# Block-sparse attention with a fused feed-forward on one core: sums of squares a step later, raw-query loads behind the query copies, and scores beside AV at the end of a step

## The chip, the cores and the metric

The kernel runs on one core of one Trainium2 chip. The core has five engines that run their own instruction streams and wait for each other by semaphores: TensorE (PE in the profile, with its weight loads shown apart as PEld), VectorE (DVE), ScalarE (ACT), GpSimd (POOL) and SyncE (SP), which here only issues DMAs. Transfers run on 16 DMA engines. The metric is device microseconds of one execution. A profile is one execution taken by the hardware profiler; its span runs from its first to its last instruction.

## The reference, cut to what matters

Four batches of eight heads, 768 tokens, head size 64. Queries and keys are cut into blocks of 32. A query block sees its own and its two neighbour blocks, the first and the last block, and three sampled blocks; the first and last query blocks see all. The attention output of all heads is the input of a two-layer feed-forward net.

```python
scores = scale * np.matmul(q, k.transpose(0, 1, 3, 2))
scores = np.where(mask, scores, -1000000000.0)
scores = scores - np.max(scores, axis=-1, keepdims=True)
attn = np.exp(scores)
attn = attn / (np.sum(attn, axis=-1, keepdims=True) + 1e-09)
attn_out = np.matmul(attn, v)
...
x = np.ascontiguousarray(attn_out.transpose(0, 2, 1, 3)).reshape(B * S, H * D)
h = x @ w_in                      # 3072 x 512 @ 512 x 2048
g = np.maximum(0.01 * h, h)
return (g @ w_out).astype(np.float32)
```

## The kernel before

**Numbers.** Every float32 operand is scaled by a power of two and split into two float16 halves, so that TensorE runs in float16: high times high, plus the two cross products. The scale comes from a sum of squares: ScalarE squares a raw tile with an accumulated row sum (L544 for keys, L575 for queries, L480 for values), TensorE sums the rows over the partitions by a matmul with ones (L131; tiles q_sum, k_sum, v_sum), VectorE makes the scale (L145 to L154), and then ScalarE writes the high half and VectorE the low half (L556 and L558 for keys, L582 and L584 for queries).

**Queries.** A half item of 128 query rows is loaded raw into rq (one buffer, so a load waits until the half item before has been split), split into qa, turned by a DMA transpose into qs (L587), and copied twice, with its upper and lower partitions exchanged, into qxs (L589, L590). The scores need qs and qxs. Keys go the same way into kt (transpose L562), values go through DRAM (scr) and come back gathered as vg. kg is the gathered keys of one query tile; GpSimd copies the sampled blocks into it (L644).

**Units, pairs and steps.** A unit is two heads of one 64-query tile; two units are a pair. The loop over all 192 units makes one step per unit. Twelve items (4 batches of 3) have 16 units each, so step 32 begins item 0_2 (batch 0, third item), and names read batch_item_tile_headpair. A unit runs through scores s (L702), the row minimum and scaled copy p (L711, DVE), the exponential (L723, ACT), the norm r (L734, L735), the high half pp (L750, ACT), the low half pp (L771, DVE), one DMA transpose per pair into pt (L776), and AV (L803) into the bank av. In the first item TensorE turns instead (tile turn). A tile of av is then evacuated into x.

**Feed-forward.** An item that has its four tiles makes eight chunks. A chunk is 24 matmuls h (L838), ht on ACT (L844), leaky maximum and cast g on DVE (L847, L851), the low half of g on GpSimd (L852), and 12 matmuls o (L865). The first two items run it weight quarter by weight quarter while the weights are still being decoded from float64 on ACT and DVE (tiles W and wbuf, L344 to L423); from about 230 us on the weights are there.

**What sets the order.** Each step walks through the letters of a string in CFG and emits what each letter stands for: t is L711 of this unit; d, i, s are norm, high half and low half of earlier units; x the exponential; S the scores of the next pair, in a pair's second step; c, m, g the activation of a chunk; o its second matmuls; v the evacuation; a AV of a pair whose low half was made three steps ago; p the side work on queries, keys and values; w the weights; h a chunk's first matmuls. What is emitted gets a priority by its place, and a scheduler that simulates the engines while the program is built then fixes each engine's order; so a moved letter can move other work too. Side work runs in generators that give back a cost at each yield; a step has a quota of 1.2 (1.6 in the first 16 steps), and a generator that has used it up goes on in the next step. SyncE's queue holds all direct loads, transposes and copies in one order, and a DMA whose data is not ready holds those behind it.

**What sizes the waits.** The scores have two buffers in PSUM, so a pair's scores wait until L711 has read the pair before; pt has three buffers, p four, rq one, kg and vg two, x three.

Of the kernel before, what the change touches and what calls it, by code (L numbers as in the profile page):

```python
# [43 lines left out]
    "lead0": 2,  # L44
    "ob": 4,
    "ord": "dtsixScmgovabphw",
    "p": 4,
    "pe_t": 1,
    "pp": 3,
# [19 lines left out]
def tile_block_sparse_attention_ffn(  # L69
# [19 lines left out]
    nc = tc.nc  # L89
# [129 lines left out]
    last_sp = {}  # L219
# [4 lines left out]
    def behind(begin, name):  # L224
        for i in nc.cur_bb.bb.instructions[begin:]:
            if name:
                tc.add_manual_dep(i, name, mybir.DependencyInfo(
                    mybir.DependencyClass.NoSync, mybir.DependencyReason.DATA), reason="order")
# [281 lines left out]
    def load_q(b, j, i):  # L510

        t = pa.tile([P, H, D], F32, tag="rq", name=f"rq_{b}_{j}_{i}", bufs=CFG["rq"])
        lo = j * N2 - BLOCK + i * P
        src = lambda a, n: q[b, :, a:a + n, :].rearrange("h t d -> t h d")
        if lo < 0:
            nc.sync.dma_start(out=t[:BLOCK], in_=src(0, BLOCK))
            nc.sync.dma_start(out=t[BLOCK:Q2], in_=src(S - BLOCK, BLOCK))
            nc.sync.dma_start(out=t[Q2:], in_=src(BLOCK, Q2))
        else:
            nc.sync.dma_start(out=t, in_=src(lo, P))  # L520
        return t
# [13 lines left out]
    def prep_k(b, hp, rk):  # L535

        nm = f"k{b}_{hp}"
        ss = sm.tile([P, 1], F32, tag="ssk", name=f"ss_{nm}")
        if b == 0:
            k16 = early_k.bitcast(F16)[:, (NP + hp) * 2 * S:(NP + hp + 1) * 2 * S].rearrange(  # L540
                "p (n l d) -> p n l d", n=HC, l=2)
        else:
            k16 = pa.tile([P, HC, 2, D], F16, tag="k16", name=f"k16_{nm}", bufs=1)
        nc.scalar.activation(flat(k16)[:, :S], flat(rk), AF.Square, accum_out=ss)  # L544
        yield 1.0
        yield 0.01
        pb = scale_sum(ss, 1, nm)
        yield 0.2
        inv, s = scale_of(pb, 1, nm, fl="k")
        if (b, "inv") not in kready:  # L550
            kready[b, "inv"] = cst.tile([P, NP], F32, name=f"kinv_{b}")
        nc.vector.tensor_scalar(
            out=kready[b, "inv"][:, hp:hp + 1], in0=inv[:, :1], scalar1=-SCALE, scalar2=None, op0=ALU.mult)
        yield 0.4
        raw = rk.rearrange("p h c d -> p (h c) d")
        nc.scalar.activation(k16[:, :, 1, :], raw, AF.Copy, scale=s[:, :1])  # L556
        yield 1.0
        nc.vector.scalar_tensor_tensor(  # L558
            out=k16[:, :, 0, :], in0=raw, scalar=s[:, :1], in1=k16[:, :, 1, :], op0=ALU.mult, op1=ALU.subtract)
        if b not in kts:  # L560
            kts[b] = pa.tile([P, H, S], F16, tag="kt", name=f"kt_{b}", bufs=2)
        nc.sync.dma_start_transpose(  # L562
            out=kts[b][:, 2 * hp:2 * hp + 2, :].rearrange("p h (c t) -> p (h c) t", t=P),
            in_=k16.rearrange("p n l d -> p (n l d)"))
        if b == 0:
            last_sp["k", hp] = latest()
        kready[b, hp] = True
        yield 1.2

    def prep_q(b, j, i, rq):  # L570

        nm = f"q{b}_{j}_{i}"
        ss = sm.tile([P, 1], F32, tag="ssq", name=f"ss_{nm}")
        qa = pa.tile([P, H, 2, D], F16, tag="qa", name=f"qa_{nm}", bufs=1)
        nc.scalar.activation(flat(qa)[:, :H * D], rq.rearrange("p h d -> p (h d)"), AF.Square, accum_out=ss)  # L575
        yield 0.7
        yield 0.01
        pb = scale_sum(ss, 1, nm)
        yield 0.2
        inv, s = scale_of(pb, 1, nm)  # L580
        yield 0.4
        nc.scalar.activation(qa[:, :, 1, :], rq, AF.Copy, scale=s[:, :1])  # L582
        yield 0.7
        nc.vector.scalar_tensor_tensor(  # L584
            out=qa[:, :, 0, :], in0=rq, scalar=s[:, :1], in1=qa[:, :, 1, :], op0=ALU.mult, op1=ALU.subtract)
        qs = pa.tile([P, H, P], F16, tag="qs", name=f"qs_{nm}", bufs=2)
        nc.sync.dma_start_transpose(out=qs, in_=flat(qa))  # L587
        qxs = pa.tile([P, H, P], F16, tag="qxs", name=f"qxs_{nm}", bufs=2)
        nc.sync.dma_start(out=qxs[:D], in_=qs[D:])  # L589
        nc.sync.dma_start(out=qxs[D:], in_=qs[:D])  # L590
        last_sp["q"] = latest()
        qstack[b, j, i] = (qs, qxs, inv)
        yield 0.8
# [329 lines left out]
    def until(key, ready):  # L923
        while not ready():
            assert next(gens[key], "end") != "end" or ready(), key
# [84 lines left out]
    def get_q(n):  # L1010
        if n < len(halves):
            if n >= CFG["rq"]:
                until(("q", *halves[n - CFG["rq"]]), lambda: halves[n - CFG["rq"]] in qstack)
            rq[n] = load_q(*halves[n])

    def start_q(n):
        if n < len(halves):
# [59 lines left out]
    step = 0  # L1077
# [44 lines left out]
    for u in units:  # L1122
# [33 lines left out]
        if step == 0:  # L1156
            scores([u])
        c = aq[0] if aq else None
        for w in CFG["ord"]:
            if w == "c" and c:  # L1160
                ffn_act1(c)
            elif w == "m" and c:
# [130 lines left out]
```

## Time and profile before

| | |
|---|---|
| three runs | 866.07 us median (863.73 to 870.84) |
| the profiled execution | 863.27 us, span 861.6 us |
| mean granted TensorE clock | 0.948 |
| VectorE busy | 598.1 us in 1595 instructions |
| ScalarE busy | 512.4 us in 1199 instructions |
| GpSimd busy | 353.5 us in 472 instructions |
| DMA | 135.33 MB, mean 157 GB/s, q1 (SyncE's queue) 64.9% of 16 engines' span |

The span falls into three parts. Up to about 230 us the weights are loaded and decoded, attention of batch 0 runs beside it, and TensorE's granted clock swings between full and half. From 230 us to about 800 us one attention step and half a feed-forward chunk alternate on TensorE. The last 60 us are the last items' feed-forward alone. In a view of waits, a row gives the waiting engine and line, what it waited for, the total, the number and the longest. In a timeline, a row gives start, duration, engine, line, operation, tiles and count, and in brackets the idle time before it. A view of windows gives each engine's busy time per stretch, then the granted clock and the share of DMA.

### The profile page before, as it was taken

The numbers are of one execution on the slowest core, as the hardware profiler recorded it, in microseconds if no ns is written. First come the engines' busy times: TensorE is split into PE (matmuls) and PEld (weight loads), VectorE is DVE, ScalarE is ACT, GpSimd is POOL, SyncE is SP. The second block draws the span as 40 slices with busy tenths as digits, with TensorE's granted clock in tenths as the row PEclk, the third lists the DMA queues.
The fourth block names the chain that finished last, engine by engine and source line by source line (L and its number), as shares of the span: only waits on it lengthen the run. The fifth ranks groups of instructions, "written<-read, shape, count | busy, mean of one in ns | idle before, by whom it ended". The sixth has DMA issues, their size and how long they took to land.

```text
span 861.6 us, 20081 instructions
## 1 busy us (share of the span) xinstructions
PE 753.5 (87%) x7140; PEld 499.7 (58%) x7140; DVE 598.1 (69%) x1595; ACT 512.4 (59%) x1199; POOL 353.5 (41%) x472
## 2 busy tenths in 40 slices
PE   2676695768997998998999889989999999999997
PEld 1465464455655565665666566656666656666664
DVE  5788997998786785667775667578677666753221
ACT  5777676884545667666556656667557475553211
POOL 0227562623243354554433354363534554532121
PEclk9977786898999999999999999999999999999999
DMA  9988399996828979968949898887688595655000
GB/s 221 245 254 242 76 182 243 256 268 121 176 54 176 174 157 188 218 135 156 190 93 183 171 167 186 170 147 180 146 145 154 118 160 142 132 120 87 26 1 25
DMA packets 312003, 135.33 MB, mean 157 GB/s; under 512 B 279773, under 2 KB 292062, under 8 KB 311902
## 3 DMA queue, kind: packets, MB, share of 16 engines
q1 hardware_dynamic: 305262, 113.59, 64.9%
q0 software_dynamic: 6640, 20.45, 9.4%
q8 instruction: 56, 0.92, 0.5%
q14 instruction: 45, 0.37, 0.1%
HBM read 65.58 MB, written 12.58 MB: 91 GB/s over the span
## 4 chain that ended last, share of the span: by engine, by line
PE 52%; DMA 19%; DVE 16%; ACT 6%; issue 4%; SPq 2%; POOLq 0%; POOL 0%; ACTq 0%; DVEq 0%
PE h L838 20%; PE o L865 19%; PE av L803 5%; DMA qs_q<-qa_q 5%; PE s L702 5%; DMA pt<-pp 4%; DVE pp L771 3%; DMA qxs_q<-qs_q 3%; DMA kt<-k_k 3%; DVE p L711 2%; ACT p L723 2%; DMA wbuf<-in_moe_w_out_dram 2%; DVE W L353 2%; DMA v<-in_v_dram 1%; PE turn L761 1%
## 5 line engine op out<-in xcount | busy, mean ns | idle before, releaser
L865 PE MATMUL o<-W,g 128*128 128x512 f16 x1152 | 275.9, 386 | 5.2 <-DVE ob L886 3.4
L838 PE MATMUL h<-x,W 128*128 128x256 f16 x2304 | 275.1, 276 | 0.0
L838 PEld LDWEIGHTS <-W 128*128 128x128 f16 x2304 | 223.9, 100 | 44.5 <-issue 9.5
L852 POOL TENSOR_TENSOR g<-ht,g 128x512 f16<-128x512 f32 x96 | 116.7, 1215 | 295.3 <-DVE g L851 260.9
L865 PEld LDWEIGHTS <-g 128*128 128x128 f16 x1152 | 109.0, 99 | 131.0 <-issue 18.9
L723 ACT ACTIVATE p<-p,mx 128x384 f32<-128x384 f32 x208 | 126.0, 606 | 90.7 <-DVE mx L711 63.7
L644 POOL COPY kg<-kt 128x256 f16 x264 | 133.2, 530 | 67.9 <-PE s L702 41.3
L771 DVE SCALAR_TENSOR_TENSOR pp<-p,r,pp 128x384 f16<-128x384 f32 x188 | 123.7, 686 | 29.7 <-ACT pp L750 28.6
L711 DVE CUSTOM_DVE_ANT_0 p<-s,em,nsc 128x384 f32<-128x384 f32 x176 | 102.5, 610 | 24.8 <-PE s L702 20.2
L750 ACT ACTIVATE pp<-p,r 128x384 f16<-128x384 f32 x188 | 104.3, 604 | 26.1 <-DVE r L735 15.5
L847 DVE SCALAR_TENSOR_TENSOR ht<-ht 128x512 f32<-128x512 f32 x96 | 67.8, 706 | 71.2 <-ACT ht L844 70.8
L671 POOL DMA_INDIRECT vg<-scr,rows x88 | 93.9, 1067 | 46.7 <-issue 18.3
L803 PE MATMUL av<-pt,vg 128*64 128x128 f16 x2112 | 83.0, 229 | 17.5 <-DVE top L448 7.8
L803 PEld LDWEIGHTS <-vg 128*64 128x64 f16 x2112 | 70.4, 115 | 46.2 <-issue 39.5
L844 ACT ACTIVATE ht<-h,gd 128x512 f32<-128x512 f32 x80 | 54.2, 678 | 69.8 <-PE h L838 55.3
L702 PE MATMUL s<-kg,qs_q 128*64 128x384 f16 x352 | 62.6, 348 | 23.8 <-DVE mx L711 20.7
L702 PE MATMUL s<-kg,qxs_q 128*64 128x384 f16 x352 | 61.0, 341 | 12.1 <-DMA qxs_q<-qs_q 12.1
L702 PEld LDWEIGHTS <-qs_q 128*64 128x64 f16 x416 | 26.8, 111 | 54.7 <-issue 39.8
L851 DVE CAST g<-ht 128x512 f16<-128x512 f32 x96 | 41.8, 436 | 10.1 <-PE o L865 8.3
L735 DVE RECIPROCAL r<-sum 128x2 f32<-128x2 f32 x96 | 15.4, 160 | 40.4 <-ACT sum L734 38.9
L723 ACT ACTIVATION_READ_ACCUMULATOR p<-p,mx 128x1 f32 x208 | 39.0, 188 | 0.0
L575 ACT ACTIVATE qa_q<-rq 128x512 f16<-128x512 f32 x25 | 15.7, 627 | 38.2 <-DMA rq<-in_q_dram 38.1
(138 smaller groups left out, 767.9 us busy)
## 6 DMA issues: line engine op xcount, KB each, us to landing
vg<-scr SPq DMA_DIRECT2D x33, 256.0 KB
qxs_q<-qs_q SPq DMA_DIRECT2D x48, 128.0 KB
v<-in_v_dram SPq DMA_DIRECT2D x32, 192.0 KB
scr<-v SPq DMA_DIRECT2D x16, 384.0 KB
W<-in_moe_w_in_dram SPq DMA_DIRECT2D x5, 1024.0 KB
rq<-in_q_dram SPq DMA_DIRECT2D x20, 256.0 KB
out_dram<-ob SPq DMA_DIRECT2D x20, 256.0 KB
rk<-in_k_dram SPq DMA_DIRECT2D x24, 192.0 KB
```

What stands on the lines that cost most here:

```text
L644: nc.gpsimd.tensor_copy(out=kg[:, :, slot * BLOCK:(slot + 1) * BLOCK], in_=kt[:, :, bass.ds(off, BLOCK)])
L671: nc.gpsimd.indirect_dma_start(out=vg[:n_, c, :], out_offset=None, in_=scr[b][:, :], in_offset=bass.IndirectOffsetOnAxis(ap=rows[:n_, c - ...
L702: nc.tensor.matmul(o, a, k, start=(n == 0), stop=(n == 1)))
L711: nc.vector.tensor_tensor_reduce(out=u.p[i], in0=u.sp[i], in1=kgs[u.b, u.T][1] if u.T else zero.to_broadcast([P, KEYS]), scale=u.nsc, scal ...
L723: nc.scalar.activation(u.p[i], u.p[i], AF.Exp, scale=-1.0, bias=u.mx[:, :1], accum_out=u.pair.sum[:, u.pi, i:i + 1])
L750: nc.scalar.activation(pp[:, 0, :], p, AF.Copy, scale=u.r)
L771: nc.vector.scalar_tensor_tensor(out=pp[:, 1, :], in0=p, scalar=u.r, in1=pp[:, 0, :], op0=ALU.mult, op1=ALU.subtract)
L803: nc.tensor.matmul(o, a, m, start=(c == 0 and l == 0), stop=(c == n - 1 and l == 1)))
L838: nc.tensor.matmul(c.ph[:, i], w, x, start=(d == 0 and m == 0), stop=(d == NP - 1 and m == 2)))
L847: nc.vector.scalar_tensor_tensor(out=c.t, in0=c.t, scalar=0.01, in1=c.t, op0=ALU.mult, op1=ALU.max)
L852: nc.gpsimd.tensor_tensor(out=c.g[:, 1], in0=c.t, in1=c.g[:, 0], op=ALU.subtract)
L865: nc.tensor.matmul(o, a, w, start=(c.first and i == 0 and m == 0), stop=(c.last and i == 1 and m == 2)))
```

## The change

Three edits. The square of a raw key or query tile of batches 1 to 3 now gives back a cost of 1.25, above a step's quota, so that the matmul with ones is emitted a step later. From the fourth half item on, the load of the next raw query tile stands, on SyncE's queue, behind the last emitted exchange copy of queries. And from step 32 on the order string is another: S and a, the scores of the next pair and AV, stand side by side at the end of the step.

```diff
@@ -44,6 +44,8 @@
     "ord": "dtsixScmgovabphw",
+    "ord1": "dtsixcmgovbphwSa",
+    "ord1_at": 32,
@@ -542,7 +544,7 @@
         nc.scalar.activation(flat(k16)[:, :S], flat(rk), AF.Square, accum_out=ss)
-        yield 1.0
+        yield 1.25 if b else 1.0
@@ -573,7 +575,7 @@
         nc.scalar.activation(flat(qa)[:, :H * D], rq.rearrange("p h d -> p (h d)"), AF.Square, accum_out=ss)
-        yield 0.7
+        yield 1.25 if b else 0.7
@@ -1011,7 +1013,10 @@
                 until(("q", *halves[n - CFG["rq"]]), lambda: halves[n - CFG["rq"]] in qstack)
+            begin = len(nc.cur_bb.bb.instructions)
             rq[n] = load_q(*halves[n])
+            if n > 2:
+                behind(begin, last_sp["q"])
@@ -1156,7 +1161,7 @@
         c = aq[0] if aq else None
-        for w in CFG["ord"]:
+        for w in CFG["ord1" if step >= CFG["ord1_at"] else "ord"]:
```

No instruction is added or removed; what changes is where instructions stand. Lines of the changed kernel are 2 higher than those named above up to the load of raw queries, and 5 higher behind it.

First place, TensorE in the steady stretch, item 2_2, the end of the scores of a pair (s_2_2_0_0) and what follows. The first fence is the kernel before, the second the changed one.

```order
L702 MATMUL s_2_2_0_0_0_9657<-kg1_99,qs_q2_2_0_9336 64x384
L702 LDWEIGHTS qxs_q2_2_0_9338
L702 MATMUL s_2_2_0_0_0_9657<-kg1_99,qxs_q2_2_0_9338 64x384
L702 LDWEIGHTS qxs_q2_2_0_9338
L702 MATMUL s_2_2_0_0_0_9657<-kg1_99,qxs_q2_2_0_9338 64x384
L838 LDWEIGHTS W_96
L838 MATMUL h_2_0_8_9696<-x_2_0_8205,W_96 128x256
```

```order
L704 MATMUL s_2_2_0_0_0_9684<-kg1_99,qs_q2_2_0_9334 64x384
L704 LDWEIGHTS qxs_q2_2_0_9336
L704 MATMUL s_2_2_0_0_0_9684<-kg1_99,qxs_q2_2_0_9336 64x384
L704 LDWEIGHTS qxs_q2_2_0_9336
L704 MATMUL s_2_2_0_0_0_9684<-kg1_99,qxs_q2_2_0_9336 64x384
L805 LDWEIGHTS vg1_101
L805 MATMUL av_2_1_2_0_9696<-pt_2_1_2_1_9421,vg1_101 64x128
```

Where the scores were followed by feed-forward matmuls on the whole array (128 columns of weights), they are now followed by AV, which like the scores uses 64 columns. Counted over TensorE's whole order from the first scores of step 32 on, the stream goes 134 times from a matmul on 128 columns to one on 64 before, and 108 times now.

Second place, SyncE around the query transpose of half item 2_1_1 (qs_q2_1_1), before and then changed.

```order
L776 DMA_TRANSPOSE pt_2_1_0_3_8960<-pp_2_1_0_2_8835 128x12x128
L587 DMA_TRANSPOSE qs_q2_1_1_8767<-qa_q2_1_1_8579 128x8x128
L520 DMA rq_2_2_0_8772<-in_q_dram 128x8x64
L664 DMA vg0_100<-scr_2_6911 128x1024
L589 DMA qxs_q2_1_1_8769<-qs_q2_1_1_8767 64x1024
L590 DMA qxs_q2_1_1_8769<-qs_q2_1_1_8767 64x1024
```

```order
L589 DMA_TRANSPOSE qs_q2_1_1_8767<-qa_q2_1_1_8579 128x8x128
L778 DMA_TRANSPOSE pt_2_1_0_3_8960<-pp_2_1_0_2_8835 128x12x128
L591 DMA qxs_q2_1_1_8769<-qs_q2_1_1_8767 64x1024
L592 DMA qxs_q2_1_1_8769<-qs_q2_1_1_8767 64x1024
L522 DMA rq_2_2_0_8772<-in_q_dram 128x8x64
L666 DMA vg0_100<-scr_2_6911 128x1024
```

The raw load and the load of vg went behind the two copies, and the transpose of pp, which stood ahead of the query's, now stands between it and its copies.

Third place, VectorE where item 0_2 begins, in the weight stage: what stands around the first L711 of step 32 (p_0_2_0_0), before and then changed.

```order
L771 SCALAR_TENSOR_TENSOR pp_0_1_3_2_2252<-p_0_1_3_3_0_2187,r_0_1_3_2_2243,pp_0_1_3_2_2252 128x384
L200 ISA wi2_sq_2437,wi2_ss_2454<-wi2_sq_2437,eye_87 128x128
L200 ISA wi2_ss_2454 128x1
L847 SCALAR_TENSOR_TENSOR ht_0_0_4_2507<-ht_0_0_4_2507 128x512
L711 ISA p_0_2_0_0_0_2246,mx_0_2_0_0_2247<-s_0_2_0_0_0_2197,em_0_8_2193,nsc_0_2_0_0_2195 128x384
L711 ISA mx_0_2_0_0_2247 128x1
```

```order
L425 SCALAR_TENSOR_TENSOR W_96<-W_96,wo1_s_2141 128x2x512
L773 SCALAR_TENSOR_TENSOR pp_0_1_3_0_2156<-p_0_1_3_0_0_2018,r_0_1_3_0_2147,pp_0_1_3_0_2156 128x384
L773 SCALAR_TENSOR_TENSOR pp_0_1_3_0_2156<-p_0_1_3_1_0_2049,r_0_1_3_0_2147,pp_0_1_3_0_2156 128x384
L713 ISA p_0_2_0_0_0_2246,mx_0_2_0_0_2247<-s_0_2_0_0_0_2197,em_0_8_2193,nsc_0_2_0_0_2195 128x384
L713 ISA mx_0_2_0_0_2247 128x1
L713 ISA p_0_2_0_1_0_2296,mx_0_2_0_1_2297<-s_0_2_0_1_0_2198,em_0_8_2193,nsc_0_2_0_0_2195 128x384
L713 ISA mx_0_2_0_1_2297 128x1
L560 SCALAR_TENSOR_TENSOR k16_k1_0_2093<-rk_1_0_1864,k1_0_s_2264,k16_k1_0_2093 128x12x64
```

Step 32's L711 came forward on VectorE, ahead of the low halves of pair 0_1_3_2, the squares of wi2 and the key split.

## The prediction

> **What bounds the kernel now.** I read the page's busy shares and its chain first, then windows by stage, then TensorE's waits in the stage that is longest, and last timelines at the places that the change moves.
>
> ```profile
> span 861.6 us, 20081 instructions
> PE 753.5 (87%) x7140; PEld 499.7 (58%) x7140; DVE 598.1 (69%) x1595; ACT 512.4 (59%) x1199; POOL 353.5 (41%) x472
> PE 52%; DMA 19%; DVE 16%; ACT 6%; issue 4%; SPq 2%; POOLq 0%; POOL 0%; ACTq 0%; DVEq 0%
> ```
>
> Windows: engine busy times in the order of the page's first line, then clock, DMA share, GB/s.
>
> ```profile
> 150.00:230.00 80.00, 63.20 (x628) 42.01 (x627) 74.02 (x198) 56.12 (x122) 29.46 (x32) 0.89 0.94 211
> 230.00:430.00 200.00, 186.75 (x1755) 121.92 (x1754) 144.50 (x382) 121.08 (x294) 91.63 (x127) 0.98 0.81 160
> 430.00:620.00 190.00, 179.19 (x1753) 116.52 (x1752) 131.25 (x356) 118.67 (x286) 84.44 (x113) 0.98 0.80 162
> 620.00:800.00 180.00, 176.53 (x1773) 116.50 (x1772) 114.28 (x295) 104.86 (x254) 76.64 (x102) 1.00 0.66 129
> ```
>
> The reader is to see two kernels in one. In the weight stage, whose last part the first row shows, VectorE (74 of 80 us) and the DMA engines (0.94) are full and TensorE is not. From 230 us to 800 us TensorE is busy 542.5 of 570 us and nothing else is near full. There only two things can shorten the time: less time on TensorE, or fewer of its waits. These are its waits from 230 us to the end:
>
> ```profile
> PE s L702 <- DMA qxs_q<-qs_q: 10.1, 7, 3.2
> PE av L803 <- DMA pt<-pp: 5.8, 4, 1.9
> PE s L702 <- DVE mx L711: 3.7, 4, 2.1
> PE k_sum L131 <- ACT k_k L544: 3.5, 3, 2.6
> PE av L803 <- issue: 2.4, 1, 2.4
> PE o L865 <- DVE g L851: 1.6, 1, 1.6
> ```
>
> Together 27.1 us: the most that moving waits alone can give.
>
> **The change part by part.** *Scores beside AV.* TensorE's own cost of going between 128 and 64 columns, from its timeline (start, duration):
>
> ```profile
> 605.60 2.76 PE L865 MATMUL o<-W,g 128*128 128x512 f16 x12
> 608.20 2.78 PE L838 MATMUL h<-x,W 128*128 128x256 f16 x24
> 610.82 1.03 PE L865 MATMUL o<-W,g 128*128 128x512 f16 x4
> ...
> 622.15 0.33 PE L702 MATMUL s<-kt,qs_q 128*64 128x384 f16 x2
> 622.31 0.33 PE L702 MATMUL s<-kt,qxs_q 128*64 128x384 f16 x2
> 622.58 2.79 PE L838 MATMUL h<-x,W 128*128 128x256 f16 x24
> ...
> 636.55 2.78 PE L838 MATMUL h<-x,W 128*128 128x256 f16 x24
> 639.27 1.53 PE L803 MATMUL av<-pt,v 128*64 128x128 f16 x48
> ```
>
> Twenty-four h before an o take 2.62 us from start to start (608.20 to 610.82), before an av 2.72 us: 0.10 us to go in. Two s before more s take 0.16 us (622.15 to 622.31), before an h 0.27 us: 0.11 us to come out. An excursion costs 0.21 us; an exit from AV looks a little cheaper, so I take 0.19. TensorE's order has 26 excursions fewer from step 32 on (134 to 108): 26 x 0.19 = **-4.9 us**, on the path, with 26 x 0.16 and 26 x 0.21 as ends (-4.2 and -5.5).
>
> *The same letters, seen from the waits.* By these cadences (2.62/24 = 0.109 us an h, 2.60/12 = 0.216 an o, 0.16 for two s, as much for six av) I summed TensorE's work between two places of each order. From a query's q_sum to the first scores that use it stand 9.1 us of work for the second halves of items 1_2, 2_1, 2_2, 3_1 and 3_2 before, and 11.0 to 11.3 after; for 1_1 it goes from 13.7 to 16.4. These are six of the seven waits for qxs; the worst:
>
> ```profile
> 389.95 0.33 PE L702 MATMUL s<-kg,qs_q 128*64 128x384 f16 x2
> 393.43 0.35 PE L702 MATMUL s<-kg,qxs_q 128*64 128x384 f16 x2 [3.15 <-DMA qxs_q<-qs_q]
> ```
>
> With 2 us more work ahead of it this one falls to about 1.2 us and the other five, 6.0 us together, to nothing: -8 of the 10.1. Against it, item 1_0's first half, the seventh with 0.9 us, goes from 15.1 to 10.0 us of work; five us more at worst, and I take 1, since on SyncE's queue its transpose now stands ahead of the four stores of values that preceded it. Net **-7 us**, ends -10 and +5. Scores go behind h and o of their step, so L711 of the next pair starts later, but the work between a pair's scores and the reading of its buffers stays: where scores wait for L711, the shortest distance is 1.65 us in both orders, so these 3.7 us stay (0). The copies into kg wait for the scores that free it; both move together (0). AV: the two waits at item 1_0 have 18.4 and 13.8 us of work behind their scores where they had 13.9 and 12.0, and should go (about 3.8 us); those at 2_0 and 3_0 have 15.6 where they had 18.1, but their transpose no longer waits behind a load of vg, and I leave them. The 2.4 us at 2_0_2 have 27.3 us for 23.1, and go; the wait for g has its o elsewhere now: 1 us. Sum -3.8 - 2.4 - 1.0, of which I take **-6 us** (ends -9 and +3).
>
> *Feed-forward behind the scores' letters.* An o needs ht, the maximum, the cast and the low half of its h:
>
> ```profile
> L852 POOL TENSOR_TENSOR g<-ht,g 128x512 f16<-128x512 f32 x96 | 116.7, 1215 | 295.3 <-DVE g L851 260.9
> L847 DVE SCALAR_TENSOR_TENSOR ht<-ht 128x512 f32<-128x512 f32 x96 | 67.8, 706 | 71.2 <-ACT ht L844 70.8
> L844 ACT ACTIVATE ht<-h,gd 128x512 f32<-128x512 f32 x80 | 54.2, 678 | 69.8 <-PE h L838 55.3
> L851 DVE CAST g<-ht 128x512 f16<-128x512 f32 x96 | 41.8, 436 | 10.1 <-PE o L865 8.3
> ```
>
> That is 3.0 us; between a chunk's h and its o stands 6.7 us of other TensorE work at the least in the steady stretch, so 3.7 us of delay are covered (0).
>
> *Raw loads behind the copies.* On SyncE's queue, at item 1_2:
>
> ```profile
> 384.12 1.23 SPq L587 DMA_TRANSPOSE qs_q<-qa_q  x1
> 385.41 0.58 SPq L516 DMA_DIRECT2D rq<-in_q_dram  x1
> 386.04 0.46 SPq L517 DMA_DIRECT2D rq<-in_q_dram  x1
> 386.55 0.69 SPq L518 DMA_DIRECT2D rq<-in_q_dram  x1
> 389.37 0.49 SPq L589 DMA_DIRECT2D qxs_q<-qs_q  x1
> ```
>
> The loads are issued in the shadow of the transpose: the queue stands idle from 387.24 to 389.37 until qs has landed. Moving them saves no issue time, only the data that stood ahead of the copies; in the tight places a transpose of pp takes their room. 0 for the copies, beyond the distances already counted. The load itself starts 3 to 5 us later, and ScalarE, whose square waits for it, holds the activations behind it:
>
> ```profile
> ACT qa_q L575 <- DMA rq<-in_q_dram: 31.7, 15, 5.3
> ```
>
> Two us a time today, no wait of an o comes of it, by the 3.7 us of cover: 0, and some us if the wait doubles. [...] The load of vg that follows goes behind the copies too; its tile has two buffers and is wanted a tile later (0).
>
> *Sums a step later.* The cost is meant to give the square time before TensorE's k_sum waits for it. In the order it hardly does: from the sum of the head pair before to k2_2's sum stand 10.3 us of work where 11.8 stood, to k3_2's 9.1 where 9.4 stood, so the 3.5 us do not go: **+1 us** (ends -3.5 and +3).
>
> *The clock.* Half-speed windows follow waits:
>
> ```profile
> 391.00:398.00 7.00, 4.57 (x28) 3.35 (x29) 3.89 (x15) 4.81 (x12) 0.09 (x1) 0.76 1.09 176
> 485.00:492.00 7.00, 4.63 (x28) 1.88 (x27) 3.30 (x9) 3.91 (x11) 3.40 (x4) 0.82 0.99 244
> ```
>
> 0.24 of 7 us lost is 1.7 us. The 0.98 of 230 to 620 us is four such places. Two lose their wait: **-3.4 us**. [...]
>
> *The weight stage.* Item 0_2 begins in it. The work that VectorE has ahead of the last weights' scale is some 3 us less in the new order, counted at the row means, but queries 0_2_0, 0_2_1 and 1_0_0 have 8.5, 12.1 and 10.0 us of TensorE work before their scores where they had 14.3, 17.0 and 15.1. I take 0 (ends -3.5 and +27.5, below).
>
> *New waits.* The order before has 27.1 us of them after 230 us, and a new one will not be free of its own. I give back a seventh of that, **+4 us**, a choice and no reckoning.
>
> Sum: -4.9 - 7 - 6 + 1 - 3.4 + 4 = -16.3 us. The profiled execution took 863.27 us, span and 1.7 us around it; it lies 2.8 us below the median of 866.07. From the median: 866.1 - 16.3 = **850 us**, faster by 1.9%. About 1% (8.7 us) is what a measurement of this kernel can tell from no change.
>
> **The rivals.** *The waits only move.* What the new order takes from qxs and AV it finds elsewhere, and only excursions are saved: 866.1 - 4.9 = 861 us. For it: the k_sum distances above, pp transposes in the loads' old place, and that TensorE's waits have six sources. Against it: six of seven qxs waits gain 2 us of cover. That the sums' edit does nothing is part of it.
>
> *Slower, by the weight stage.* VectorE takes its instructions in order, and step 32's L711 now stands ahead of weight work. If query 0_2_0's copies come late, L711 waits and the decode behind it. Before, this chain was:
>
> ```profile
> 127.13 8.60 SPq L587 DMA_TRANSPOSE qs_q<-qa_q  x1
> ...
> 140.72 0.54 SPq L589 DMA_DIRECT2D qxs_q<-qs_q  x1
> ```
>
> From the transpose's issue to the copies' is 13.6 us, and from there to the scores 4.1 us as at item 1_2 (389.37 to 393.43): 17.7 us, against 8.5 us of work now. That is 9.2 us, and at most the same again for 0_2_1 and 1_0_0: 27.5 us if nothing else covers it. 866.1 - 16.3 + 27.5 = 877 us; it decides from 25 us on. Against it: the transpose of pp that stood behind the issue of 8.6 us now stands ahead of it, so that AV 0_1_2 can start earlier, and the engines that wait here have slack in TensorE's case (63 of 80 us).
>
> *All waits named go*, and the clock stays up: 866.1 - 4.9 - 10 - 9 - 3.5 - 6.8 = 832 us.
>
> **How the numbers follow.** Forecast 0.60, waits only move 0.25, slower 0.09, all go 0.06. The range is 838 to 868: it leaves out the two outer cases, 0.15 together, and holds the first two with the nearer ends of their terms. Of the forecast and the best case all, and of the second rival little, lie under 857.4: faster 0.65; same 0.26; slower 0.09.
>
> **What would show it.** TensorE's qxs waits after 230 us under 4 us, AV's under 3 us, k_sum's unchanged near 3.5 us, two half-clock windows fewer there, and h-to-av and s-to-h starts as quoted. The last weights' sum near 221 us would show the weight stage unchanged. The forecast is wrong if that comes 5 us later, if ScalarE's wait for rq grows past 60 us and o waits for g, or if the sum of TensorE's waits after 230 us stays above 22 us.

## The result, and the profile after

The changed kernel is slower: 874.27 us median against 859.56 us for the kernel before in the same session, ratio 1.0156 (95% interval 1.0127 to 1.0186). That is 13.4 us by the ratio and 14.7 us between the medians. The forecast was 850 us, 1.9% faster than the 866.07 us known then.

Ratios leave out executions more than 1.5% above the quickest of their kernel; these kernels scatter (standard deviation 4.5 us over 29 executions of the kernel before), so this cuts some ordinary ones too, and below the median over all stands beside each ratio; where few are left (two of six for the 0.9879 near the end) the median is the safer of the two. A trace is one execution: the two profiled ones, 863.27 and 870.46 us, lie only 7.2 us apart, one above its kernel's median and one below, so a trace says where, and the ratios how much.

The page of the changed kernel, span and engines:

```profile
span 868.8 us, 20085 instructions
PE 750.8 (86%) x7140; PEld 502.5 (58%) x7140; DVE 608.4 (70%) x1595; ACT 510.3 (59%) x1199; POOL 349.1 (40%) x472
```

TensorE has a little less to do and 7 us more span to do it in; VectorE has 10 us more. The windows in the three steady stretches (columns as before):

```profile
230.00:430.00 200.00, 184.23 (x1714) 120.75 (x1711) 148.85 (x386) 120.83 (x285) 86.52 (x119) 0.97 0.81 164
430.00:620.00 190.00, 179.18 (x1780) 119.89 (x1774) 135.20 (x360) 120.81 (x295) 84.57 (x117) 0.98 0.81 164
620.00:800.00 180.00, 173.00 (x1755) 116.43 (x1754) 122.57 (x303) 103.05 (x256) 79.56 (x105) 0.99 0.65 133
```

The granted clock is 0.97, 0.98, 0.99 where it was 0.98, 0.98, 1.00. These rows are rounded; in narrower windows the half clock (0.50) shows in four places and 13.7 us before (at 278, 394, 490 and 571 us) and in five places and 23.9 us now (at 259, 399, 525, 587 and 706 us), so 6.8 us were lost to it and now 12.0. Each of these stretches begins within a wait of TensorE or less than 1 us behind it, of 1.79, 3.15, 2.37 and 2.09 us before and 4.60, 5.00, 2.69, 2.75 and 2.74 us now; before, the waits of 2.32 and 2.64 us at 333 and 511 us had none behind them. TensorE's waits from 230 us to the end, changed kernel (total, times, longest):

```profile
PE s L704 <- DMA qxs_q<-qs_q: 14.3, 6, 5.0
PE s L704 <- DVE mx L713: 7.6, 8, 1.4
PE o L867 <- DVE ob L888: 4.6, 1, 4.6
PE o L867 <- POOL g L854: 1.7, 2, 0.9
PE h L840 <- ACT x L821: 1.4, 1, 1.4
PE o L867 <- DVE g L853: 1.0, 2, 0.8
PE k_sum L133 <- issue: 0.8, 1, 0.8
PE av L805 <- DMA pt<-pp: 0.8, 1, 0.8
```

The AV waits are nearly gone (0.8 us for pt, was 5.8, and nothing in place of the 2.4 at 2_0_2), k_sum's too (0.8, were 3.5). The waits for the exchanged queries are 14.3 us where they were 10.1, those for L713 (here the mx row) 7.6 where they were 3.7, and a wait for ob is new. With two small rows not shown the sum is 32.9 us where it was 27.4.

How far one trace can be trusted shows in the held string, a kernel below that was traced twice. Its instructions stand in the same order in both traces on TensorE, VectorE, ScalarE and SyncE. The waits for qxs are 9.6 us in the second, and in the first:

```profile
PE s L710 <- DMA qxs_q<-qs_q: 15.4, 7, 4.0
```

Its waits for mx are 2.7 and 3.3 us. So a difference of 4 us in the waits for qxs between two traces shows no growth; that they did not fall to 3 us it does show. The last weights' sum:

```profile
L133 PE MATMUL wo_sum<-wo_ss,ones x8: 250/260/271, 89.1 to 223.6; 128*128 128x1 f32 x8
```

It starts at 223.6 us, 2.1 us later than in the trace before (221.5). The 7.2 us between the traces add up so: work in TensorE's order -5.0 (counted at the prediction's prices), waits after 230 us +5.5, clock +5.1, weight stage +2.1, together +7.7. The other half of the 13 to 15 us is the scatter of these two executions: one lies 3.7 us above its median, the other 3.8 below.

### The profile page after: what moved, and what is told of

It reads as the page before. It is cut to its first block, busy times and chain, and to the rows that moved or that the text cites. A ratio compares the mean times of both kernels' runs of the same rounds, so it can differ in the third digit from the quotient of the medians.

```text
span 868.8 us, 20085 instructions
## 1 busy us (share of the span) xinstructions
PE 750.8 (86%) x7140; PEld 502.5 (58%) x7140; DVE 608.4 (70%) x1595; ACT 510.3 (59%) x1199; POOL 349.1 (40%) x472
## 5 line engine op out<-in xcount | busy, mean ns | idle before, releaser
L867 PE MATMUL o<-W,g 128*128 128x512 f16 x1152 | 279.3, 389 | 9.2 <-DVE ob L888 4.6
L840 PEld LDWEIGHTS <-W 128*128 128x128 f16 x2304 | 227.4, 100 | 48.2 <-issue 7.9
L773 DVE SCALAR_TENSOR_TENSOR pp<-p,r,pp 128x384 f16<-128x384 f32 x188 | 134.6, 743 | 26.9 <-ACT pp L752 26.1
L646 POOL COPY kg<-kt 128x256 f16 x264 | 129.5, 516 | 59.5 <-PE s L704 29.8
L713 DVE CUSTOM_DVE_ANT_0 p<-s,em,nsc 128x384 f32<-128x384 f32 x176 | 103.2, 610 | 31.8 <-PE s L704 28.1
L805 PE MATMUL av<-pt,vg 128*64 128x128 f16 x2112 | 80.7, 229 | 5.5 <-DMA vg<-scr,rows 2.3
L805 PEld LDWEIGHTS <-vg 128*64 128x64 f16 x2112 | 73.0, 116 | 20.7 <-issue 12.0
L577 ACT ACTIVATE qa_q<-rq 128x512 f16<-128x512 f32 x25 | 15.7, 627 | 57.4 <-DMA rq<-in_q_dram 57.4
L704 PEld LDWEIGHTS <-qxs_q 128*64 128x64 f16 x416 | 25.5, 114 | 32.0 <-DMA qxs_q<-qs_q 23.0
```

Source lines behind the costliest of these rows:

```text
L646: nc.gpsimd.tensor_copy(out=kg[:, :, slot * BLOCK:(slot + 1) * BLOCK], in_=kt[:, :, bass.ds(off, BLOCK)])
L704: nc.tensor.matmul(o, a, k, start=(n == 0), stop=(n == 1)))
L713: nc.vector.tensor_tensor_reduce(out=u.p[i], in0=u.sp[i], in1=kgs[u.b, u.T][1] if u.T else zero.to_broadcast([P, KEYS]), scale=u.nsc, scal ...
L773: nc.vector.scalar_tensor_tensor(out=pp[:, 1, :], in0=p, scalar=u.r, in1=pp[:, 0, :], op0=ALU.mult, op1=ALU.subtract)
L805: nc.tensor.matmul(o, a, m, start=(c == 0 and l == 0), stop=(c == n - 1 and l == 1)))
L840: nc.tensor.matmul(c.ph[:, i], w, x, start=(d == 0 and m == 0), stop=(d == NP - 1 and m == 2)))
```

## The experiments

Each edit has a switch of its own, so most kernels below are one line of the changed kernel set back. "Ratio" is to the kernel before in the same session.

**One edit at a time.** Order string alone, later sums alone, raw loads alone, and string with loads, by setting the other parts back:

```diff
-    "ord1_at": 32,
+    "ord1_at": 999,
...
-        yield 1.25 if b else 1.0
+        yield 1.0
...
-        yield 1.25 if b else 0.7
+        yield 0.7
...
-            if n > 2:
+            if n > 999:
```

The first pair takes the new string away, the next two the later sums, the last one the loads behind the copies.

> The kernel before with the new order string from step 32 alone. Theory A (three separate harms, one from each edit): the string saves its excursions (133 to 105 by the order, 28 x 0.19 = 5.3 us) and the AV waits, but puts the two low halves of pp between the scale instructions of a query on VectorE in five second half items, so their chains grow by the 2 us that TensorE's order gains: qxs waits after 230 us stay 8 to 12 us, no transpose of pp stands between a query's transpose and its copies there (4.5 to 6 us from one to the other), o never waits 4 us for ob. Span 3 to 8 us under the kernel before, ratio 0.991 to 0.997. Theory B (ScalarE, held by late raw loads, is the cause): all the loss is in the loads, so this one shows the forecast gain, ratio under 0.985. Theory C (the string itself harms, by L713 coming late): ratio above 1.005, waits of s for mx above 7 us.

> The kernel before with the later sums alone. Theory A: six loads of vg go ahead of the last key transpose of batch 1, kt lands some 7 us after its issue, VectorE's copies into kg wait for it and o waits 4 to 5 us for ob near 255 us; k_sum waits fall by 2 us or so. Ratio 1.001 to 1.006. Theories B and C: no difference, 0.998 to 1.002.

> The kernel before with the raw loads behind the copies alone. Theory A: without the new string the transpose of pp does not come between a query's transpose and its copies in the tight second half items (a load of vg does), so their waits for qxs stay within 2 us of the 10.1 before; ScalarE waits longer for rq (45 to 60 us in all) and nothing on TensorE comes of it. Ratio 0.999 to 1.004. Theory B: ScalarE's wait reaches TensorE as waits for mx and g, 5 us more of them, ratio 1.006 or more. Theory C: 0.998 to 1.002.

> The changed kernel without the later sums. Theory A: the transpose of pp stands between the query's transpose and its copies in four tight second half items, 7 us from one to the other instead of 5.5, so waits for qxs are 12 to 16 us; the wait for ob near 255 us is gone. 5 us under the changed kernel: ratio to the kernel before 1.006 to 1.012. Theory B: as the changed kernel, 1.012 to 1.018. Theory C: as the string alone.

| kernel | ratio (95%) | medians, us |
|---|---|---|
| string alone | 1.0060 (1.0019 to 1.0100) | 867.15 / 861.54 |
| later sums alone | 1.0052 (1.0013 to 1.0091) | 866.19 / 861.54 |
| loads alone | 1.0041 (0.9998 to 1.0084) | 865.15 / 861.54 |
| string and loads | 1.0151 (1.0078 to 1.0224) | 875.26 / 861.54 |

No edit gains. The three losses sum to 1.53% (0.60 + 0.52 + 0.41) against 1.56% for all three, but that they add is not shown: string and loads together already lose 1.51%, so by these ratios the later sums add nothing there, and the interval of the loads alone holds 1. Theory A is right on the later sums, at the edge on the loads, and wrong on the string, which should have gained; there C had the ratio and the waits for mx, and C is wrong on the later sums, which it held for harmless. String and loads lie where theory B had them and above A's range (their interval reaches into it), though their wait for qxs is 10.3 us, not the 12 to 16 of A. The later sums lose what A said, but in their trace o waits only 1.4 us for ob: the place of their loss is not shown to be the one named. Nor do they take away the waits that they were made for, those of k_sum:

```profile
PE k_sum L133 <- ACT k_k L546: 4.9, 2, 3.0
```

They were 3.5 us in the kernel before and are 0.8 with the string alone, so it is not the later sums that removed them. The string's trace, TensorE's waits from 230 us on:

```profile
PE s L704 <- DMA qxs_q<-qs_q: 10.5, 5, 3.8
PE s L704 <- DVE mx L713: 8.3, 6, 3.0
PE h L840 <- ACT x L821: 6.3, 1, 6.3
PE o L867 <- POOL g L854: 3.5, 4, 1.8
PE av L805 <- DMA pt<-pp: 2.8, 1, 2.8
```

The third row is new. ScalarE's timeline at that place, item 1_1 (start, duration, and in brackets the idle time ahead):

```profile
328.70 0.28 ACT L736 ACTIVATE sum<-sum,floor 128x2 f32<-128x2 f32 x1
337.68 0.84 ACT L546 ACTIVATE k_k<-rk 128x768 f16<-128x768 f32 x1 [8.69 <-DMA kt<-k_k]
338.43 0.19 ACT L546 ACTIVATION_READ_ACCUMULATOR k_k<-rk 128x1 f32 x1
338.52 0.40 ACT L821 ACTIVATE x<-xf 128x256 f16<-128x256 f32 x1
```

ScalarE stands 8.7 us at the square of a raw key, whose target is still being read by the transpose of the key before. Nothing needs that square yet. But x, an instruction of 0.4 us whose xf VectorE has ended at 328.81 us, is queued behind it, and the first h of item 1_0 needs x.

**Clearing the query chain.** The changed kernel, with the loads behind the copies only after the weight stage; with the low halves of pp ordered behind the last query scale; with the transposes of pp ordered behind the last query copies; and with both:

```diff
-            if n > 2:
+            if n > 7:
```

```diff
         inv, s = scale_of(pb, 1, nm)
+        last_sp["qs"] = latest()
...
+        begin = len(nc.cur_bb.bb.instructions)
         for p, pp in zip(u.p, u.pp):
...
+        behind(begin, last_sp.get("qs"))
```

```diff
         last_sp["p"] = latest()
+        behind(len(nc.cur_bb.bb.instructions) - 1, last_sp.get("q"))
```

> The changed kernel, with the raw loads behind the copies only from item 1_1 on, after the weight stage. Theory D (the loads harm in the weight stage, where query 0_2_1's copies come late): the waits of s for qs and qxs between 130 and 232 us, 8.8 us in the changed kernel, fall to 2 us or less, and the time by 3 to 5 us: ratio to the kernel before 1.009 to 1.013, against 1.0156 of the changed kernel. Theory E (they harm in the steady stretch, by ScalarE's waits or by the transpose of pp that takes their place): the ratio stays 1.014 to 1.018, the last sum of the weights at the same place.

> The changed kernel, with the low halves of pp ordered behind the last query scale on VectorE. Theory A (the low halves within the scale's chain cost the chain 2 us in five second half items): from a query's sum to its high half 1.5 to 2.5 us there instead of 3.8 to 4.2, waits for qxs after 230 us 7 to 11 us instead of 14.3; the transpose of pp still stands between the query's transpose and its copies. Ratio 1.008 to 1.013. Rival F (the waits only move: whatever the chain gains, exponentials, maxima and o lose): qxs waits fall, those for mx and g rise by as much, 1.014 to 1.018.

> The changed kernel, with each transpose of pp ordered behind the last emitted query copies on SyncE, the low halves left where they are. Theory A: from a query's transpose to its copies 5 to 5.7 us in the second half items 1_2, 2_1, 2_2, 3_1 instead of 7.0, waits for qxs 8 to 11 us instead of 14.3; AV may wait 2 us more for pt. Ratio 1.009 to 1.014. Rival F: 1.014 to 1.018, what qxs gains AV waits for pt.

> The changed kernel with both orders, low halves behind the query scale and transposes of pp behind the copies; TensorE has 13.3 us of work between the sum and the scores there instead of 10.7. Theory A: waits for qxs after 230 us under 4 us, and half-clock windows with them: 10 to 14 us under the changed kernel, ratio 0.998 to 1.005. Rival F: waits for qxs under 4 us too, but 1.010 or more.

| kernel | ratio (95%) | medians, us |
|---|---|---|
| loads late | 1.0062 (1.0013 to 1.0110) | 870.87 / 862.85 |
| low halves behind the scale | 1.0152 (1.0100 to 1.0205) | 875.41 / 862.85 |
| transposes behind the copies | 1.0281 (1.0219 to 1.0343) | 885.34 / 862.85 |
| both | 1.0202 (1.0140 to 1.0263) | 878.94 / 862.85 |

Theory A falls here, and rival F's 1.010 or more holds for both orders. The low halves alone change nothing (qxs waits 14.1 us; from sum to high half the chain became shorter in two of the four places looked at, and not in 1_2 and 2_2). The transposes behind the copies alone are the slowest kernel: waits for qxs fall to 7.9 us, but AV waits 12.1 us for pt and the scores 10.7 for mx. With both orders the wait for qxs almost goes, as forecast, and the kernel is no faster than the changed one. The chain is no shorter for it: from q_sum to the issue of the copies it takes 12.0 us in the mean of the second half items 1_2, 2_1, 2_2, 3_1 and 3_2, as in the changed kernel, so what removed the wait looks to be the longer cover (13.3 us of TensorE's work). The waits from 232 us on with both orders:

```profile
PE s L705 <- DVE mx L714: 19.0, 8, 3.9
PE k_sum L133 <- ACT k_k L546: 4.9, 2, 3.9
```

Waits for qxs are 2.8 us there, those for L713 (here L714) 19.0. One of them is followed here, at 604 us, where TensorE waits 3.44 us. ScalarE, then VectorE, then TensorE of that kernel:

```profile
593.06 0.51 ACT L652 ACTIVATE em<-mask 128x384 bf16<-128x384 f32 x1
597.61 0.63 ACT L577 ACTIVATE qa_q<-rq 128x512 f16<-128x512 f32 x1 [4.05 <-DMA rq<-in_q_dram]
598.15 0.18 ACT L577 ACTIVATION_READ_ACCUMULATOR qa_q<-rq 128x1 f32 x1
598.24 0.28 ACT L737 ACTIVATE sum<-sum,floor 128x2 f32<-128x2 f32 x1
```

```profile
598.55 0.17 DVE L738 RECIPROCAL r<-sum 128x2 f32<-128x2 f32 x1 [4.16 <-ACT sum L737]
```

```profile
603.88 0.53 PE L705 MATMUL s<-kg,qs_q 128*64 128x384 f16 x2 [3.44 <-DVE mx L714]
```

Again ScalarE stands at a square, this time until a raw query lands. The sum behind it releases VectorE 4.16 us late, and with the delay VectorE reaches the next L714 at 603.21, behind its other work; the scores wait for that. The late loads gave a smaller ratio, below theory D's range (by medians 1.0093, inside it), and the queries' waits in the weight stage went (none of 8.8 us left), but waits of AV for pt of 11.4 us took their place there and the last weights' sum came at 229 us, so the time did not come from where D puts it.

**Holding the squares.** Both traces point at squares that ScalarE reaches long before they are needed: in the trace before, the square of a second half item runs, from item 1_1 on, 45 to 52 us ahead of its q_sum. An order given for ScalarE alone holds those of batches 1 to 3:

```diff
                 u.p[i], u.p[i], AF.Exp, scale=-1.0, bias=u.mx[:, :1], accum_out=u.pair.sum[:, u.pi, i:i + 1])
+        last_sp["exp"] = latest()
...
+        begin = len(nc.cur_bb.bb.instructions)
         nc.scalar.activation(flat(k16)[:, :S], flat(rk), AF.Square, accum_out=ss)
+        if b:
+            behind(begin, last_sp.get("exp"))
```

and the same three lines at the query square. The order is given for ScalarE alone, but the scheduler then places all engines anew: between the traces of the changed kernel without and with the hold, TensorE's order differs in 52 places and VectorE's in 132, about as much as between the string alone and the changed kernel (54 and 138). So the hold is not a change on ScalarE alone.

> The changed kernel, with the squares of raw keys and queries of batches 1 to 3 held on ScalarE behind the last exponential emitted before them, some 12 instructions later than the scheduler put them. Theory B (ScalarE stands at those squares until a DMA lands, and the sum, x and high halves behind them come late to VectorE, to L713 and so to the scores): ScalarE's waits for rq and for kt between 232 and 820 us, 48.0 and 11.8 us in the changed kernel, fall under 10 us together, TensorE's waits for mx, x and g from 11.7 us to under 6, ratio to the kernel before 1.003 to 1.010. Rival G (ScalarE has slack, waits just turn up elsewhere): its waits for DMAs fall as much, the ratio stays 1.013 to 1.018.

> The kernel before with the same squares held. Theory B: ScalarE's waits for rq and kt, 31.7 and 15.5 us in that stretch, fall under 8 us together, and TensorE's waits for mx, pt, g with them: ratio 0.990 to 0.997. Rival G: 0.998 to 1.003.

> The changed kernel with the raw loads behind the copies only from item 1_1 on, and the squares held. Theories B and D together: the two gains add, ratio 0.996 to 1.003. D alone: as without the hold, 1.004 to 1.011. Neither: 1.012 to 1.018.

> The order string alone, with the squares held. Theory B: the wait of h for x behind a key square (6.3 us in the run of the string alone) goes, and that for mx falls from 8.3 to under 5: ratio 0.994 to 1.001. Rival G: 1.003 to 1.009.

| kernel | without the hold | with it (95%) | medians with it, us |
|---|---|---|---|
| changed | 1.0156 | 0.9954 (0.9909 to 0.9998) | 859.18 / 861.80 |
| string alone | 1.0060 | 0.9916 (0.9874 to 0.9957) | 855.73 / 861.80 |
| before | 1 | 1.0018 (0.9980 to 1.0056) | 863.50 / 861.80 |
| changed, loads late | 1.0062 | 1.0048 (1.0012 to 1.0083) | 865.34 / 861.80 |

This is the largest gain of the study: 2.0% on the changed kernel, 1.4% on the string, with ratios below theory B's ranges in both. On the kernel before it is nothing that can be measured, against B; there too the waits for rq go (31.7 us to none), while those for kt stay (14.4 us of 15.5). ScalarE's DMA waits between 230 and 870 us, changed kernel first, then with the hold:

```profile
ACT qa_q L577 <- DMA rq<-in_q_dram: 48.0, 16, 5.5
ACT k_k L546 <- DMA kt<-k_k: 11.8, 6, 3.3
```

```profile
ACT k_k L547 <- DMA kt<-k_k: 4.5, 2, 2.7
ACT pp L759 <- DMA pt<-pp: 3.9, 2, 2.3
```

The 48.0 us for rq are gone. TensorE's waits for mx stay (7.8 us), so that part of B's path is not what the hold saves in the changed kernel; those for qxs are 9.6, those for ob nothing, and the clock in the three stretches after 230 us is 0.99, 0.99 and 1.00. (This trace, 851.38 us, lies 8 us below its kernel's median.) The kernel with late loads gains almost nothing by the ratios and 0.5% by the medians, and no trace here says why.

**Which squares, and what the other edits cost under the hold.** On the string alone, only query squares or only key squares held; and the string with the hold, plus later sums or plus loads:

> The order string alone, with only the query squares held. Theory Bq (the early query squares, for which ScalarE waited 14 times and 21.6 us in the run of the string alone, are what costs): ratio to the kernel before 0.990 to 0.997, as with both held (0.9916). Theory Bk (the key squares, 6 waits and 19.7 us, one of 8.7 us with the wait of h for x behind it): 1.002 to 1.008, as with none held (1.006). Both half: 0.996 to 1.002.

> The order string alone, with only the key squares held. Theory Bk: 0.990 to 0.997 and no wait of h for x above 2 us. Theory Bq: 1.002 to 1.008. Both half: 0.996 to 1.002.

> The order string and the later sums, with the squares held. Theory H (the later sums cost by the loads of vg that go ahead of a key transpose at item 1_0, hold or no hold): 0.4 to 0.5% slower than the string with the hold, ratio 0.994 to 0.999. Theory K (with the square late its sum needs the step, and the edit is worth its k_sum waits): 0.986 to 0.992.

> The order string and the raw loads behind the copies, with the squares held. Theory L (the late loads cost only by ScalarE, which no longer waits for them): as the string with the hold, ratio 0.988 to 0.994. Theory M (they cost by the weight stage's queries or by the transposes of pp that take their place): 0.3% or more slower, 0.995 to 1.001.

| kernel | ratio (95%) | medians, us |
|---|---|---|
| string, queries held | 0.9971 (0.9932 to 1.0010) | 856.79 / 860.75 |
| string, keys held | 0.9991 (0.9953 to 1.0028) | 859.76 / 860.75 |
| string, both held, later sums | 0.9948 (0.9913 to 0.9983) | 857.66 / 860.75 |
| string, both held, loads | 0.9968 (0.9924 to 1.0012) | 857.66 / 860.75 |

Holding either kind gains about half of it: 0.9 and 0.7% of the string's 1.4. The two other edits gain nothing on top of the held string; the ratios fall where theories H and M put them, but their intervals reach into that of the held string, so under the hold their loss is not shown.

**The weight stage.** The held string again, and with the string only from step 48 on:

```diff
-    "ord1_at": 32,
+    "ord1_at": 48,
```

> The order string with the squares held once more, beside the next kernel on one chip: ratio 0.988 to 0.996 if the 0.9916 holds; after the last weights' sum a stretch some 9 us shorter than in the kernel before (623.8 us from that sum to the last h), TensorE's waits for mx, x and g there under 6 us together.

> The same, but the new string only from step 48 on, so that item 0_2 in the weight stage keeps the old one. Theory W (the string also harms in the weight stage, by L713 of step 32 ahead of the weights' decode): the last weights' sum comes 4 us earlier or more, ratio 0.980 to 0.988. Against it: the weight stage is indifferent to the string, 0.988 to 0.996.

The held string gave 0.9879 (0.9801 to 0.9957; medians 858.37 and 860.71, or 0.9973), from step 48 on 0.9977 (0.9936 to 1.0018; 862.57). Leaving the string out of the weight stage does not help: theory W falls, and the last weights' sum, forecast 4 us earlier, comes at 244.8 us, more than 10 us later than in the held string. Over both sessions the held string is faster than the kernel before by 0.3 to 0.7% in medians and 0.8 to 1.2% in ratios. TensorE's waits from 230 us on in its second trace:

```profile
PE s L710 <- DMA qxs_q<-qs_q: 9.6, 6, 2.7
PE s L710 <- DVE mx L719: 3.3, 3, 1.8
PE s L710 <- DMA qs_q<-qa_q: 2.4, 2, 1.8
PE k_sum L133 <- ACT k_k L547: 2.4, 1, 2.4
```

Those for mx fell from 8.3 to 3.3 us, that of h for x from 6.3 to none. Where the hold saves and where it costs, by the traces (the last weights' sum, and the stretch from it to TensorE's last matmul, us):

| kernel | last sum, without the hold | with it | stretch, without | with it |
|---|---|---|---|---|
| before | 221.5 | 228.3 | 633.8 | 619.9 |
| string alone | 221.2 | 234.4 and 233.5 | 639.0 | 624.7 and 617.8 |
| changed | 223.6 | 220.0 | 638.8 | 623.4 |

Behind the weight stage all three kernels are some 14 us or more shorter with the hold, the kernel before too. In the weight stage the hold costs the first two 7 and 12 us or more, and the changed kernel nothing. One kernel's two traces differ by 7 us in the stretch, so this is a sign and no measure of sizes.

## Why the prediction was wrong, step by step

- *Excursions, -4.9.* Right as far as the traces tell. The order's work is 5.0 us less by the prediction's prices, what is left of the 7.2 us between the traces is -5.5, and the trace has the cheaper step, 0.17 us from the last two scores to AV where scores to h took 0.27:

```profile
387.06 0.33 PE L704 MATMUL s<-kg,qxs_q 128*64 128x384 f16 x2
387.23 1.51 PE L805 MATMUL av<-pt,vg 128*64 128x128 f16 x48
```

- *qxs waits, -7.* Wrong: +4.2 in these traces, of which the growth is within the scatter shown above; that the waits did not fall is clear of it. The step that failed is "With 2 us more work ahead of it this one falls": it counted TensorE's work from q_sum to the scores and took the chain of the query as fixed. From q_sum to the issue of the copies, in the mean of the second half items 1_2, 2_1, 2_2, 3_1 and 3_2, the chain takes 9.6 to 10.2 us in the four kernels with the old string and 11.0 to 12.6 us in all those with the new one (10.2 and 12.0 in the kernel before and the changed one). It grew by about as much as the cover. At item 1_2 it went from 13.7 to 17.8 us, from q_sum to the scores. VectorE of the changed kernel there:

```profile
384.68 0.15 DVE L149 TENSOR_SCALAR q_ex<-q_tot 128x1 int32<-128x1 int32 x1
384.77 1.99 DVE L773 SCALAR_TENSOR_TENSOR pp<-p,r,pp 128x384 f16<-128x384 f32 x1
386.69 0.14 DVE L155 TENSOR_SCALAR q_inv<-q_ex 128x1 f32<-128x1 f32 x1
386.75 0.68 DVE L773 SCALAR_TENSOR_TENSOR pp<-p,r,pp 128x384 f16<-128x384 f32 x1
387.35 0.15 DVE L156 RECIPROCAL q_s<-q_inv 128x1 f32<-128x1 f32 x1
```

  Two low halves stand between the small scale instructions, where none stood: 3.8 us from q_sum to the high half, were 1.5. In five of the second half items from 230 us on low halves stand there now, in none before. And SyncE:

```profile
389.07 1.23 SPq L589 DMA_TRANSPOSE qs_q<-qa_q  x1
390.41 2.10 SPq L778 DMA_TRANSPOSE pt<-pp  x1
396.08 0.47 SPq L591 DMA_DIRECT2D qxs_q<-qs_q  x1
```

  7.0 us from the query's transpose to its copies, were 5.2, and 7.2 and 7.0 us at 2_2 and 3_1, were 5.6 and 5.9. The prediction had 0 for the copies beyond the distances counted; they come 1.1 to 1.8 us later at these three places. That the transpose of pp is the cause is not shown. In the held string no such transpose stands there, and the first of its two traces has at 1_2:

```profile
389.56 1.23 SPq L595 DMA_TRANSPOSE qs_q<-qa_q  x1
396.65 0.49 SPq L597 DMA_DIRECT2D qxs_q<-qs_q  x1
```

  These are 7.1 us; in its second trace, with the same order, the step takes 4.7. The changed kernel with the hold does have the transpose there, and takes 5.5. The low halves within the scale could have been read from the order of VectorE beforehand; the second place of the change had shown the transposes.
- *That these waits are worth their length.* The deeper error. With both orders 11.5 us of qxs waits go and 11.4 come back at L713, and the kernel is no faster (1.0202, was 1.0156). This is the rival "the waits only move", had at 0.25; the measured time lies above its 861 us, for costs that it did not have either: more of L713's waits, more half clock, and the terms below.
- *Raw loads, 0, and ScalarE's holds, 0.* This step failed too: "Two us a time today, no wait of an o comes of it". ScalarE's waits for rq grew from 31.7 to 48.0 us, and two traces show that such a wait reaches TensorE, not by o but by what is queued behind the square: x in the string alone, the sum in the kernel with both orders. In the changed kernel itself no trace shows that path, since its waits for mx stay under the hold. Holding the squares is worth 1.4% (12 us) under the string and 2.0% (17 us) under all three edits. How much of that is ScalarE standing still, and how much the new order of the other engines, is not shown. Nor is it shown that the old string hides these waits: in its trace, too, the hold shortens the stretch behind the weights, and what it loses there is time in the weight stage. The loads alone measured +0.4%, about 3.5 us, with an interval that reaches no change.
- *Sums a step later, +1.* Mis-sized: alone +0.5%, about 4.5 us. The k_sum waits stayed, as forecast, with the later sums alone (4.9 us), and are 0.8 us with the string alone. New in the changed kernel is the wait for ob at 255 us. Six loads of vg now stand ahead of the last key transpose of batch 1 on SyncE, with four gathers on GpSimd's queue around it, and VectorE's copy into kg waits 4.79 us for kt, with ob behind it:

```profile
252.83 0.08 DVE L713 DVE_READ_ACCUMULATOR2_ANT mx<- 128x1 f32 x1
257.70 0.43 DVE L637 COPY kg<-kt 128x1024 f16<-128x1024 f16 x1 [4.79 <-DMA kt<-k_k]
```

  The later sums alone have the same six loads there, and o waits 1.4 us for ob: the loads by themselves do not make this wait.
- *AV, -6.* Right: pt 5.8 to 0.8 and the 2.4 us at 2_0_2 to 0 make -7.4 us; waits for g went from 1.6 to 2.7. *L711 stays, 0.* Wrong by +3.9. *Clock, -3.4.* Wrong, +5.1: the waits that it was to follow did not go; four stretches of half clock went with waits of 1.79 to 3.15 us, and now five go with waits of 2.69 to 5.00 us. *Weight stage, 0.* +2.1, inside its ends; the rival that put the loss there is not what happened, and the string from step 48 on is no better. *Give-back, +4.* The new waits for mx, ob, x and g are 11 us.

Of the signs under "What would show it" that were to make the forecast wrong, one came: TensorE's waits after 230 us are 32.9 us (22 was the limit). The two others did not: the last weights' sum comes 2.1 us later, not 5, and ScalarE waits 57.4 us for rq over the whole span, not 60.

What stays open: how the 13 to 15 us divide among the longer chain, ScalarE's squares and the clock; how much of the hold's gain comes from the instructions that it moved on other engines; why the hold gains nothing measurable in the kernel before although its trace is shorter behind the weights; why late loads help without the hold and not with it; and where the later sums lose when they stand alone.

## What to carry to other kernels

Cover is a difference of two distances. When an order gives a wait more work of the waiting engine, go through every other queue of its chain in the new order as well, and look for what now stands between two links. Look in an engine's order for instructions that wait for a DMA long before anyone needs them, as the query squares of the kernel before, 45 to 52 us ahead of their q_sum, and for what stands behind them: with the string alone x stood behind such a wait of 8.69 us, and TensorE waited 6.29 us for x. On TensorE, busy 536.4 of the 570 us from 230 to 800 us in the changed kernel and waiting for several other engines and DMAs, the lengths of the waits didn't add up to a gain: with both orders 11.5 us of qxs waits went, and the ratio was 1.0202 where it was 1.0156. And where one kernel's traces differ by 6 us in a single kind of wait (here 15.4 and 9.6 us for qxs), trace it twice before a wait is called longer or shorter.

## What was not expected of the hardware

The low half at 384.77 us takes 1.99 us, against a mean of 0.69 in the kernel before. GpSimd in that stretch of the changed kernel:

```profile
384.49 0.74 POOL L646 COPY kg<-kt 128x256 f16 x2
385.19 1.14 POOL L854 TENSOR_TENSOR g<-ht,g 128x512 f16<-128x512 f32 x1
386.29 0.72 POOL L646 COPY kg<-kt 128x256 f16 x1
```

Over the whole changed kernel, 85 of the 188 low halves run beside such copies and additions of GpSimd and take 0.90 us in the mean; the other 103 take 0.61. The one above is 1.3 us longer than the mean of 0.69. What makes a low half longer beside GpSimd is not shown, and this one ends at 386.76 us, before GpSimd's last copy does at 387.01. All low halves of pp together take 134.6 us in the changed kernel and 123.7 before, 133.2 with the string alone, and 123.6 with the later sums alone: it is the string that made them longer, by about 10 us of VectorE's time that the prediction did not have. They are no measure of the loss: the held string has 138.3 us of them and is faster.
